# Attention and a squared-ReLU MLP on one core: two-unit cycles start two pairs earlier, and a batch's first product moves into the next batch's first two cycles

## Chip, core and metric

One core of one Trainium2 chip. The metric is the device time of one execution in microseconds, the median of several runs. The kernel before takes 417.85 us (417.56 to 418.05, four runs).

## The reference

```python
# q, k, v: 8 batches, 12 heads, 448 queries, 64 wide;  w_in: 768 x 2048;  w_out: 2048 x 768
scores = (1 / sqrt(64)) * q @ k.T
m = max(scores)                                   # by row
e = exp(scores - m)
attn = e / (sum(e) + exp(-m) + 1e-09)             # a "one" more in the denominator
x = (attn @ v)  as 3584 tokens x 768              # (batch, query) x (head, width)
out = relu(x @ w_in) ** 2 @ w_out
```

With exp(m) multiplied through, the denominator is the sum of exp(scores) plus one. The kernel computes it so, without the maximum.

## The kernel before, as far as the change touches it

A *unit* is a pair of heads with 448 queries (batch 0's are split into 192 and 256 queries). Per unit: eight score matmuls (in two halves, `c` = 0 and 1, two score tiles each), four exponentials on ScalarE, three adds on VectorE that shorten the row sums, values, row sums by TensorE, and a reciprocal made of two ScalarE instructions. The `..._psum` pools below hold TensorE's result tiles in PSUM, its result memory; a buffer can be written again once its reader is done. The *first product* (x @ w_in, 16 tiles of a batch's 448 tokens) and the *second product* (a *whole tile* is 128 tokens by 384 columns, 16 *pieces*) fill TensorE's time between them.

```python
s_psum = ctx.enter_context(tc.tile_pool(name="s_psum", bufs=2, ...))   # score tiles, 2 banks each
x_psum = ctx.enter_context(tc.tile_pool(name="x_psum", bufs=1, ...))
m_psum = ctx.enter_context(tc.tile_pool(name="m_psum", bufs=3, ...))
z_pool = ctx.enter_context(tc.tile_pool(name="z", bufs=2))             # reciprocals
...
def row_sums(us, sums):
    ...                                            # matmuls with ones into zp
    rcp = z_pool.tile([128, 512], FP32, name="rcp")
    nc.scalar.activation(out=rcp[:, 0:m], in_=zp[:, 0:m], func=AF.Ln, bias=one_b)
    nc.scalar.activation(out=rcp[:, 0:m], in_=rcp[:, 0:m], func=AF.Exp, scale=-1.0)
    return rcp
...
# one-unit cycles: batch 1, all six pairs (units 12 to 17)
for i in range(2 * NPAIR, 3 * NPAIR):
    ...                                            # scores, first product of batch 0, values, sums
    for step in range(3):
        add_chunks(u, et, es, half, step)          # VectorE's three adds
        drain(share[0] * (0.15, 0.1, 0.15)[step])  # some first product
    ...
# two-unit cycles: batches 2 to 7, three cycles each (pr = 0, 2, 4)
for c in range((NU - 3 * NPAIR) // 2):
    ...
    scores(ua, ea, 0)
    rows(11)                                       # 11 pieces of second product
    scores(ua, ea, 1)
    ...
    rows(11)
    scores(ub, eb, 0)
    ...
    rows(10)
    scores(ub, eb, 1)
    ...                                            # values and normalising of the cycle before
    if pr == 0:
        run(ins, len(ins))
        queue((b - 1) * S, S)                      # first product of the batch before
        if b > 2:
            run(outs)                              # one whole tile of second product
        ...
    n, early = ((3, 0 if b > 2 else 1), (7, 3), (6, 3))[pr // 2]
    run(ins, early)                                # tiles of first product
    for at in (i, i + 1):
        rcps[at] = row_sums([units[at]], (ess.pop(at)[0:1],))
    run(ins, n - early)
    if pr == NPAIR - 2:
        complete(b * S)                            # its second product may now start
```

## Time and profile before

| | before |
|---|---|
| median, us | 417.85 |
| span of the profiled execution, us | 415.9 |
| TensorE busy | 405.5 us (98%) |
| ScalarE busy | 238.4 us (57%) |
| start of batch 3, us | 116.53 |
| one batch in the steady part, us | 47.50 |
| from the last cycle's end (last values) to the end, us | 61.83 |

### The profile page before, as it was taken

What the parts mean: (1) busy time and instruction counts of PE and PEld (TensorE: products, weight loads), DVE (VectorE), ACT (ScalarE), POOL (GpSimd) and SP (SyncE); (2) the same over time, 40 slices, a digit from 0 to 9 for tenths busy, and PEclk for the clock granted to TensorE, in tenths of its full rate; (3) what the DMA queues carried; (4) which work ended last, traced back from release to release, by engine and by line L of the source; (5) the groups of instructions that cost most, each with busy time, mean ns of one, the idle gap of its engine ahead of it and who ended that gap; (6) DMA issues with size and microseconds to landing.
All of it is one profiled execution on the core that took longest, in us unless ns stands there. A gap on an engine that the chain in (4) does not pass through costs nothing.

```text
span 415.9 us, 10695 instructions
## 1 busy us (share of the span) xinstructions
PE 405.5 (98%) x4721; PEld 256.7 (62%) x4721; DVE 278.8 (67%) x535; ACT 238.4 (57%) x329; POOL 36.4 (9%) x58
## 2 busy tenths in 40 slices
PE   8889999899999999999999999999999999999997
PEld 3567666566566666665666666665666666555664
DVE  4769888768865868568766769658676669287000
ACT  4897998664675664673576564674666655100111
POOL 7523220020000200002000400001000000000000
PEclk9999999999999999999999999999999999999999
DMA  9999999889109790199509871198101101010222
GB/s 201 197 197 198 200 197 223 159 120 199 40 2 182 139 192 6 44 199 191 123 2 164 167 151 37 39 186 154 46 2 39 39 2 39 39 39 0 77 76 77
DMA packets 75823, 45.58 MB, mean 110 GB/s; under 512 B 42560, under 2 KB 72000, under 8 KB 75456
## 3 DMA queue, kind: packets, MB, share of 16 engines
q0 software_dynamic: 28848, 22.16, 35.0%
q1 hardware_dynamic: 46208, 22.05, 23.3%
q8 instruction: 37, 0.61, 0.6%
q10 hardware_dynamic: 720, 0.69, 0.6%
q14 instruction: 10, 0.08, 0.1%
HBM read 45.69 MB, written 17.93 MB: 153 GB/s over the span
## 4 chain that ended last, share of the span: by engine, by line
PE 86%; DMA 9%; ACT 2%; DVE 2%; issue 1%; POOL 0%; POOLq 0%
PE mp L284 23%; PE mp L330 17%; PE mp L286 11%; PE xp L284 8%; PE sp L199 6%; PE xp L330 6%; PE mp L234 5%; DMA kn<-in_k_dram 4%; PE xp L286 3%; DMA win<-in_moe_w_in_dram 3%; PE xp L234 3%; PE sp L187 2%; DMA vn<-in_v_dram 2%; PE mp L248 2%; ACT et L167 1%
## 5 line engine op out<-in xcount | busy, mean ns | idle before, releaser
L167 ACT ACTIVATE et<-sp 112x896 f16<-112x896 f32 (+2 forms) x192 | 165.8, 914 | 55.6 <-PE sp L199 40.1
L284 PEld LDWEIGHTS <-win 128*64 128x64 f16 x1536 | 85.3, 110 | 45.7 <-issue 2.8
L284 PE MATMUL mp<-xt,win 128*64 128x448 f16 (+2 forms) x1236 | 110.2, 324 | 1.5 <-DVE xt L263 0.8
L330 PE MATMUL mp<-wout,gs 64*128 64x384 f16 x864 | 102.3, 322 | 0.0
L330 PEld LDWEIGHTS <-gs 64*128 64x128 f16 x1152 | 56.1, 94 | 31.7
L301 DVE TENSOR_SCALAR rt<-mp 128x448 f16<-128x448 f32 (+2 forms) x99 | 61.6, 622 | 17.4 <-PE mp L284 13.3
L303 DVE TENSOR_TENSOR gs<-rt 128x448 f16<-128x448 f16 (+2 forms) x128 | 50.2, 392 | 4.4
L330 PE MATMUL xp<-wout,gs 64*128 64x384 f16 x288 | 52.6, 322 | 0.0
L251 ACT ACTIVATE rcp<-mp,one_b 128x448 f32<-128x448 f32 (+2 forms) x40 | 25.1, 629 | 40.1 <-PE mp L248 35.8
L212 DVE TENSOR_TENSOR es<-et 112x896 f16<-112x896 f16 x42 | 26.0, 620 | 17.7 <-ACT et L167 17.6
L339 ACT ACTIVATE ot<-mp 128x384 f32<-128x384 f32 (+1 forms) x29 | 14.1, 487 | 36.2 <-PE mp L286 27.6
L199 PE MATMUL sp<-qk 64*112 64x224 f16 x480 | 33.8, 260 | 0.0
L286 PEld LDWEIGHTS <-gs 128*128 128x128 f16 x256 | 24.4, 98 | 15.1 <-issue 0.4
L284 PE MATMUL xp<-xt,win 128*64 128x448 f16 x300 | 32.6, 352 | 0.0
L199 PEld LDWEIGHTS <-qk 64*112 64x112 f16 x480 | 26.3, 128 | 9.7 <-issue 5.4
L234 PEld LDWEIGHTS <-vn 112*64 112x64 f16 x432 | 22.1, 109 | 15.3 <-issue 5.2
L286 PE MATMUL mp<-wout,gs 128*128 128x384 f16 (+1 forms) x192 | 31.0, 322 | 0.0
L341 DVE SCALAR_TENSOR_TENSOR ot<-mp,ot 128x384 f32<-128x384 f32 x27 | 15.1, 558 | 21.7 <-PE sp L199 11.6
L252 ACT ACTIVATE rcp<-rcp 128x448 f32<-128x448 f32 (+2 forms) x48 | 27.7, 577 | 1.5
L214 DVE TENSOR_TENSOR es<-es,half 112x896 f16<-112x896 f16 x42 | 26.2, 625 | 1.4
L212 DVE TENSOR_TENSOR half<-et 112x896 f16<-112x896 f16 x42 | 25.9, 616 | 0.3 <-ACT et L167 0.3
L301 DVE TENSOR_SCALAR rt<-xp 128x448 f16<-128x448 f32 x29 | 18.0, 622 | 12.0 <-PE xp L286 8.3
(61 smaller groups left out, 313.9 us busy)
## 6 DMA issues: line engine op xcount, KB each, us to landing
vn<-in_v_dram POOLq DMA_DIRECT2D x7, 672.0 KB, 9.0
out_dram<-ot SPq DMA_DIRECT2D x9, 384.0 KB, 2.8
win<-in_moe_w_in_dram POOLq DMA_DIRECT2D x8, 384.0 KB, 13.9
wout<-in_moe_w_out_dram POOLq DMA_DIRECT2D x4, 768.0 KB, 12.8
stage_q<-in_q_dram POOLq DMA_DIRECT2D x4, 676.0 KB, 10.9
stage_k<-in_k_dram POOLq DMA_DIRECT2D x4, 676.0 KB, 13.3
out_dram<-ot SPq DMA_DIRECT2D x8, 288.0 KB, 3.2
out_dram<-ot SPq DMA_DIRECT2D x9, 192.0 KB, 2.7
```

What stands on the lines that cost most here:

```text
L167: nc.scalar.activation(out=out_, in_=in_, func=AF.Exp, scale=scale)
L199: nc.tensor.matmul(sp[:, odd, h * (S // 2):(h + 1) * (S // 2)], qk[r, which, kx:kx + 2 * P - 1:2], qk[r, 0, x:x + S // 2], start=True, sto ...
L212: nc.vector.tensor_add((es, half[:, 0:2 * S])[step], e[:, 2 * step], e[:, 2 * step + 1])
L214: nc.vector.tensor_add(es, es, half[:, 0:2 * S])
L234: nc.tensor.matmul(xp[64 * h:64 * h + 64, o:o + n], vns[b][:, 2 * pr + h, kk, :], of_head(chunk(et, u, kk // 2, kk), u, h), start=(kk == 0 ...
L251: nc.scalar.activation(out=rcp[:, 0:m], in_=zp[:, 0:m], func=AF.Ln, bias=one_b)
L252: nc.scalar.activation(out=rcp[:, 0:m], in_=rcp[:, 0:m], func=AF.Exp, scale=-1.0)
L284: nc.tensor.matmul(out_[x:x + 64], lhsT[:, x:x + 64], rhs, start=start, stop=stop)
L286: nc.tensor.matmul(out_, lhsT, rhs, start=start, stop=stop)
L301: nc.vector.tensor_scalar(out=rt[:, 0:m], in0=hp[:, 0:m], scalar1=0.0, scalar2=None, op0=ALU.max)
L303: nc.vector.tensor_mul(gs[:, f0:f0 + per, t0 % RING:t0 % RING + n], r, r)
L330: nc.tensor.matmul(o[:, 0:w], g[x:x + 64], wout[x:x + 64, fb, n0:n0 + w], start=(fb == 0), stop=(fb == NFFB - 1))
```

## The change

Its intent: the one-unit cycles are paced by ScalarE, and their only other work is what is left of batch 0's first product. The change shortens this stage from six units to four, and hands the last two pairs of batch 1 to the two-unit cycles, where second product fills TensorE. For there to be enough second product, a batch's first product has to be done a cycle earlier. So it all stands in the first two cycles of the next batch (8 and 8 tiles), the third has none, and the whole tile of second product goes there. VectorE's last two adds come a unit later, ahead of the sums that need them; values and sums stand before that unit's second scores and no longer behind them; and six of batch 0's 16 blocks are computed for all 448 tokens at once. The core of the diff:

```diff
-    for i in range(2 * NPAIR, 3 * NPAIR):
+    SINGLE = 2 * NPAIR + 4
+    ALONE = 10
+    def finish_sums(at):
+        for step in (1, 2):
+            add_chunks(units[at], ets[at], *ess[at], step)
+
+    for i in range(2 * NPAIR, SINGLE):
         ...
         scores(u, et, 0)
+        if not first:
+            finish_sums(i - 1)
         ...
-        drain(left() * 0.5 if first else share[0] * 0.45)
+        values(units[i - 1], ...); rcp = row_sums(...)
+        drain(left() if first else 450)
         scores(u, et, 1)
+        add_chunks(u, et, es, half, 0)
         if first:
+            normalise(done, xp, rcp)
+            queue(0, S, ALONE, NFFB)
+            queue(FIRST, S - FIRST, 0, ALONE)
+            drain(1850)
         else:
+            drain(600)
+            normalise(done, xp, rcp)
+            drain(1250)
 ... (cut: order of the loads; where the transposes stand)
-    for c in range((NU - 3 * NPAIR) // 2):
+    for c in range((NU - SINGLE) // 2):
         ...
         if pr == 0:
-            run(ins, len(ins))
             queue((b - 1) * S, S)
-            if b > 2:
-                run(outs)
-        n, early = ((3, 0 if b > 2 else 1), (7, 3), (6, 3))[pr // 2]
+        n, early = ((8, 3), (8, 3), (0, 0))[pr // 2] if c else (len(ins), 2)
         run(ins, early)
+        if c == 0:
+            normalise(units[i - 1:i], xp, rcps.pop(i - 1))
+            joined[0] = 0
+        elif pr == 4:
+            run(outs)
         for at in (i, i + 1):
             rcps[at] = row_sums([units[at]], (ess.pop(at)[0:1],))
         run(ins, n - early)
-        if pr == NPAIR - 2:
+        if c == 0 or pr == 2:
             complete(b * S)
```

More of the change, by code (lines that the diff above doesn't have):

```diff
@@ L374, with queue @@
     groups = [0]
-    def queue(t0, n):
+    def queue(t0, n, lo=0, hi=NFFB):
         per = max(1, 512 // n)
-        for f0 in range(0, NFFB, per):
+        for f0 in range(lo, hi, per):
             ns = per * DCH * n / 2.4
@@ L418 @@
     for pr in range(NPAIR):
-        transpose_at[NPAIR + 3 + pr] = (1, pr)
-    transpose_at[16], transpose_at[17] = (2, 0), (2, 1)
+        transpose_at[NPAIR + 3 + pr + pr // 3] = (1, pr)
+    SINGLE = 2 * NPAIR + 4
+    ALONE = 10
     def keep_warm(n):
@@ L463 @@
             normalise(two, xp, rcp)
-            queue(0, FIRST)
-            share[0] = left() / (NPAIR + 2)
+            queue(0, FIRST, 0, ALONE)
+            share[0] = left() / (NPAIR - 0.3)
         if i in transpose_at:
@@ L489 @@
         if i == NPAIR + 5:
+            for n0 in (0, HALF):
+                for j in range(2):
+                    load_wout(n0, j, 2)
             load_natural(2, 0, 3)
-            for j in range(2):
-                load_wout(0, j, 2)
-    for i in range(2 * NPAIR, 3 * NPAIR):
+    def finish_sums(at):
+        for step in (1, 2):
+            add_chunks(units[at], ets[at], *ess[at], step)
+    for i in range(2 * NPAIR, SINGLE):
         u, et, es, half = begin(i)
-        prev = units[i - 1]
         first = i == 2 * NPAIR
@@ L502 @@
         scores(u, et, 0)
+        if not first:
+            finish_sums(i - 1)
         if i in transpose_at:
             transposes(*transpose_at[i])
-        if i == 2 * NPAIR + 2:
-            load_natural(2, 3, 6)
-            for j in range(2):
-                load_wout(HALF, j, 2)
-            load_v(2, 0, 6)
-            stage(3)
-        drain(left() * 0.5 if first else share[0] * 0.45)
+        values(units[i - 1], ets.pop(i - 1), xp, units[i - 1][3] if first else 0)
+        done = units[i - 2:i] if first else units[i - 1:i]
+        rcp = row_sums(done, [ess.pop(units.index(d))[0:1] for d in done])
+        drain(left() if first else 450)
         scores(u, et, 1)
+        add_chunks(u, et, es, half, 0)
         if first:
-            done = units[i - 2:i]
-            values(prev, ets.pop(i - 1), xp, prev[3])
-            rcp = row_sums(done, (ess.pop(i - 2)[0:1], ess.pop(i - 1)[0:1]))
-        else:
-            done = [prev]
-            rcp = row_sums(done, (ess.pop(i - 1)[0:1],))
-            values(prev, ets.pop(i - 1), xp)
-        drain(share[0] * 0.15)
-        for step in range(3):
-            add_chunks(u, et, es, half, step)
-            drain(share[0] * (0.15, 0.1, 0.15)[step])
-        if i == 3 * NPAIR - 1 and ins and ins[0][0] < ins[0][1]:
-            run(ins)
-        normalise(done, xp, rcp)
-        if first:
-            queue(FIRST, S - FIRST)
-            share[0] = left() / (NPAIR + 1.5)
-    pending = [3 * NPAIR - 1]
-    joined[0] = 0
-    complete(S)
+            normalise(done, xp, rcp)
+            queue(0, S, ALONE, NFFB)
+            queue(FIRST, S - FIRST, 0, ALONE)
+            drain(1850)
+        else:
+            drain(600)
+            normalise(done, xp, rcp)
+            drain(1250)
+    if ins and ins[0][0] < ins[0][1]:
+        run(ins)
+    load_natural(2, 3, 6)
+    load_v(2, 0, NPAIR)
+    stage(3)
+    pending = [SINGLE - 1]
+    complete(128)
     def rows(n):
@@ L543, in rows @@
         mode[0] = COLS2
-    for c in range((NU - 3 * NPAIR) // 2):
-        i = 3 * NPAIR + 2 * c
+    for c in range((NU - SINGLE) // 2):
+        i = SINGLE + 2 * c
         b, pr = units[i][0:2]
-        new = []
-        for j in range(2):
-            new.append(begin(i + j))
-        (ua, ea, sa, ha), (ub, eb, sb, hb) = new
+        ua, ea, sa, ha = begin(i)
         scores(ua, ea, 0)
+        if c == 0:
+            finish_sums(i - 1)
         rows(11)
@@ L556 @@
         rows(11)
+        ub, eb, sb, hb = begin(i + 1)
         scores(ub, eb, 0)
@@ L563 @@
         mode[0] = COLS2
-        for at in pending:
-            if at not in rcps:
-                rcps[at] = row_sums([units[at]], (ess.pop(at)[0:1],))
-            xp = mp_tile()
-            values(units[at], ets.pop(at), xp)
-            normalise([units[at]], xp, rcps.pop(at))
+        if c == 0:
+            rcps[i - 1] = row_sums(units[i - 1:i], (ess.pop(i - 1)[0:1],))
+            xp = x_psum.tile([128, 512], FP32, name="xp")
+            values(units[i - 1], ets.pop(i - 1), xp)
+            transposes(2, 0)
+            transposes(2, 1)
+        else:
+            for at in pending:
+                xp = mp_tile()
+                values(units[at], ets.pop(at), xp)
+                normalise([units[at]], xp, rcps.pop(at))
         add_chunks(ub, eb, sb, hb, 1)
@@ L585 @@
                     stage(b + 2)
-        n, early = ((3, 0 if b > 2 else 1), (7, 3), (6, 3))[pr // 2]
+        n, early = ((8, 3), (8, 3), (0, 0))[pr // 2] if c else (len(ins), 2)
         run(ins, early)
+        if c == 0:
+            normalise(units[i - 1:i], xp, rcps.pop(i - 1))
+            joined[0] = 0
+        elif pr == 4:
+            run(outs)
         for at in (i, i + 1):
```

## The prediction

> **What bounds the kernel now.** I read first the page's table of engines, then the busy time by stretch with the cuts at the starts of the cycles, then TensorE's and ScalarE's timelines at two cycle borders, then the groups by shape.
>
> ```profile
> PE 405.5 (98%) x4721; PEld 256.7 (62%) x4721; DVE 278.8 (67%) x535; ACT 238.4 (57%) x329; POOL 36.4 (9%) x58
> ```
>
> TensorE is busy throughout, so a gain has to come out of its ten idle microseconds or out of matmuls that run slowly. The stretches say where these are (columns: span, then busy time of PE, PEld, DVE, ACT, POOL, clock, DMA share, GB/s).
>
> ```profile
> 45.13:65.40 20.27, 19.48 (x270) 13.09 (x271) 16.98 (x32) 18.93 (x26) 5.28 (x7) 1.00 1.34 199
> 67.35:83.11 15.76, 14.57 (x188) 9.51 (x186) 11.79 (x22) 10.69 (x15) 0.00 (x0) 1.00 0.87 177
> 83.11:100.83 17.72, 17.72 (x218) 11.41 (x216) 14.13 (x28) 9.58 (x13) 2.30 (x4) 1.00 1.00 175
> 100.83:116.53 15.70, 15.70 (x174) 9.32 (x172) 12.04 (x24) 9.58 (x13) 0.00 (x0) 1.00 0.15 43
> 116.53:131.45 14.92, 14.92 (x186) 9.60 (x184) 9.26 (x18) 9.96 (x14) 0.00 (x0) 1.00 0.45 73
> 131.45:148.31 16.86, 16.86 (x203) 10.68 (x201) 13.06 (x26) 9.59 (x13) 2.14 (x4) 1.00 0.97 178
> 148.31:164.03 15.72, 15.72 (x191) 9.97 (x189) 12.04 (x24) 9.58 (x13) 0.00 (x0) 1.00 0.35 83
> ```
>
> The first row is most of the one-unit cycles of batch 1 (a unit is a pair of heads, 448 queries): ACT is busy 18.93 of 20.27 us, so ScalarE is nearly the bound. The second is batch 2's first two-pair cycle, with 1.2 us of TensorE idle. From the third on TensorE never idles: the last three rows are one batch, 14.92 + 16.86 + 15.72 = 47.50 us, and every later batch repeats it. There any matmul, and any wait of a matmul, goes straight into the end. Now the border between two cycles, TensorE first, ScalarE second:
>
> ```profile
> 122.93 0.57 PE L199 MATMUL sp<-qk 64*112 64x224 f16 x8
> 123.43 1.70 PE L234 MATMUL mp<-et,vn 112*64 112x448 f16 x16
> 124.97 2.77 PE L284 MATMUL xp<-wout,gs 128*64 128x384 f16 x32
> 127.57 0.55 PE L248 MATMUL mp<-es,ones 112*64 112x448 f16 x4
> 127.95 1.30 PE L284 MATMUL mp<-xt,win 128*64 128x448 f16 x12
> 129.09 1.30 PE L284 MATMUL xp<-xt,win 128*64 128x448 f16 x12
> 130.22 1.30 PE L284 MATMUL mp<-xt,win 128*64 128x448 f16 x12
> 131.45 0.59 PE L199 MATMUL sp<-qk 64*112 64x224 f16 x8
> 133.67 0.55 PE L199 MATMUL sp<-qk 64*112 64x224 f16 x8
> ```
>
> ```profile
> 128.16 0.63 ACT L251 ACTIVATE rcp<-mp,one_b 128x448 f32<-128x448 f32 x1
> ...
> 129.95 0.58 ACT L252 ACTIVATE rcp<-rcp 128x448 f32<-128x448 f32 x1
> 131.90 1.72 ACT L167 ACTIVATE et<-sp 112x896 f16<-112x896 f32 x2 [1.36 <-PE sp L199]
> ```
>
> The row sums (L248) end at 127.95. ScalarE turns both into reciprocals, four instructions, until 129.95 + 0.58 = 130.53. Meanwhile TensorE does three tiles of the first product, 131.45 - 127.95 = 3.50 us, before the next scores. These tiles hide the reciprocals: the next exponentials find ScalarE idle for 1.36 us.
>
> **What the Trainium skill says.** "TensorE: Matmul & The Clock Gate", the table at its head, gives ScalarE a strict FIFO; so an exponential recorded after four reciprocals cannot overtake them. The trace agrees: ScalarE's starts above are in the program's order. The same page, "Back-to-back issue gap", puts a matmul at N/2.4 + 2.5 ns, 189 ns for 448 columns; here twelve 64-column halves (six products) take 129.09 - 127.95 = 1.14 us, 190 ns a product, so halves overlap and nothing is lost. "ScalarE: Activation LUTs", "What ACT_TABLE_LOAD costs", gives 186 + 0.833 N ns, 932 for N = 896; measured 914, and two in 1.72 us. "PSUM — Partial Sum Buffer", "Specifications", counts 8 banks: score tiles take 2 x 2, the value tile 1, the others 3, so a third score buffer has no room.
>
> **The change, part by part.** No arithmetic is added or removed: the built instruction orders differ only in place and shape. Four moves matter.
>
> (a) **Output work taken from the tail.** There are 19 two-pair cycles in place of 18 (32 pieces of second product each), and six extra whole tiles in place of five (16 pieces). So 32 + 16 = 48 pieces leave the tail, where 48 ran in 7.91 us: -7.8 us. They are done earlier, so this is no gain by itself; it must be set against what the earlier stages lengthen.
>
> (b) **Batch 0 and the four remaining one-unit cycles.** Batch 0's first half loses five first products of 192 columns in the cycles before (5 x 0.083 = 0.4 us); I take 0.3, so unit 12 starts at 36.9 and not 37.23. In unit 12 no product is left for the start, and the one-piece tiles need all of batch 0 normalised. Its exponentials run to 39.1, the reciprocals to 40.4, the VectorE multiply to 41.3; TensorE, done with the scores at 39.4, waits 1.9 us. Then 20 halves, and unit 13 starts at 43.3. Per unit afterwards: scores 2 x 0.5, transposes 0.42, values 0.75, sums 0.22, 28 to 30 halves about 2.8: 5.2 us, before 4.81. The late adds put two VectorE adds (2 x 0.63) in front of the sums, in line behind tile evictions of 1.0 us; I count waits of 0.7 and 0.8 us at the sums of units 13 and 14. Unit 14 starts at 48.5, unit 15 at 54.3. Unit 15 ends with 56 halves at 0.0545, 3.05 us. First two-pair cycle: 61.1.
>
> (c) **That cycle**: four score pitches with 32 pieces 6.9, sums and values 0.95, transposes 0.8, 48 halves 2.6, sums 0.4, and about 1.0 us waiting for a PSUM tile (the two-tile form uses three buffers there): it ends at 73.75. Then batch 2: its cycles have 8, 8 and 0 tiles of first product. A tile is 1.14 us. The first two are each the old row of 17.72 plus one tile, 18.86. The third is 14.92 less 3.50, about 11.45. With a border wait of 1.65 us (next paragraph) batch 3 begins at 73.75 + 1.65 + 18.86 + 18.86 + 11.45 = 124.6, before at 116.5: +8.1 us. So (a) to (c) sum to about +0.3: the work moved back in time is paid for fully.
>
> (d) **The border between a batch's third cycle and the next.** "First product in the first two cycles" takes away those three tiles. The order of the built program confirms it: second product (32 halves), sums, then scores at once; and on ScalarE four reciprocals, then six exponentials. Shift the quoted trace by 3.50 us: scores at 127.95, their exponentials wanted at 128.40, ScalarE free at 130.43. The first exponential ends at 131.35, the second at 132.2. The second pair of score tiles, due at 127.95 + 2.22 = 130.17, needs these buffers; its last four matmuls start at about 132.2, not 130.37. So TensorE stands still about 2.0 us, and later intervals of 2.17 us against 1.72 give nothing back. This comes at five borders (batches 2|3 to 6|7): +10.0 us. A batch is 18.0 + 18.0 + 11.45 + 2.0 = 49.5 in place of 47.5.
>
> Sum: +0.3 + 10.0 = 10.3, 428 us. As (b) and (c) were walked with every wait against the kernel, I take one off: **427 us**.
>
> **The rivals.** *The intended one: the stage bound by ScalarE shrinks from six units to four and TensorE fills.* For it: ScalarE's 18.93 of 20.27. If (b) and (c) had no wait at all, unit 12 to batch 3 would take 3.7 + 5.2 + 5.2 + 6.2 + 12 + 49.2 = 81.5 us, batch 3 would begin at 118.4 and, less 7.8 us, the time would be 6 us better: 412 without the border waits, 422 with them. Against it: TensorE already did 19.48 of 20.27 there. *The border wait is smaller.* If sums of the first unit come early or an eviction moves, 1 us each gives 422. *Transfers.* The second product's weights now go ahead of batch 2's queries; before, they were needed at 67.8 and now at 61.5. Four loads of 768 KB at 199 GB/s take 3.9 us each, an estimate; behind batch 1's values, which landed at about 42, they end near 58. It fits, with 3 us to spare; if it doesn't, 430.
>
> **Range and chances.** The low end, 421, is nearly all of the intended gain with most of the border waits; the high end, 431, is my walk with further waits in (b). Two per cent above is 426.2, just below my figure: slower 0.57, within 2% 0.40, faster 0.03, which would need the border waits not to exist.
>
> **What would show it.** In the new profile: each first cycle of batches 3 to 7 has idle TensorE time of about 2 us before its second scores, released by ScalarE's exponential; a batch takes 49.5 us; the tail loses 7.8 us; TensorE's idle or stretched time sits in units 12 to 15 too, and the first two-pair cycle starts near 61. The prediction is wrong if batches still take 47.5 us, if the two-pair cycles begin by 58, or if the first output rows wait for a load.

## The result, and the profile after

427.06 us (427.02 to 427.19, four runs) against 417.85: the ratio is 1.0222, 95% interval 1.0204 to 1.0239, slower. (A ratio is taken from the runs of the same rounds, so it is not quite the ratio of the medians.) The page's table of engines:

```profile
PE 406.7 (96%) x4697; PEld 264.9 (62%) x4697; DVE 280.7 (66%) x538; ACT 236.4 (56%) x328; POOL 36.2 (9%) x58
```

TensorE does the same work in a span of 425.3 us and idles eight microseconds longer. The stretches, cut at the starts of the stages, with the columns of the prediction's view:

```profile
42.11:60.41 18.30, 17.07 (x228) 10.19 (x226) 15.39 (x30) 13.56 (x18) 3.47 (x5) 1.00 1.35 202
60.41:73.45 13.04, 12.23 (x176) 8.65 (x174) 9.94 (x19) 8.40 (x12) 0.00 (x0) 1.00 1.24 217
73.45:94.34 20.89, 19.61 (x230) 13.48 (x228) 15.50 (x30) 11.70 (x17) 0.00 (x0) 1.00 0.59 115
94.34:113.20 18.86, 18.86 (x230) 12.28 (x229) 15.15 (x30) 9.59 (x13) 2.13 (x4) 1.00 0.77 148
113.20:124.69 11.49, 11.49 (x135) 7.05 (x133) 7.25 (x14) 7.54 (x10) 0.00 (x0) 1.00 0.14 36
124.69:144.53 19.84, 18.48 (x216) 13.53 (x214) 13.04 (x25) 11.78 (x18) 0.37 (x1) 1.00 0.66 125
```

They are: one-unit cycles (units 13 to 15); the first two-unit cycle; batch 2's three cycles; batch 3's first. The fourth row is a cycle with eight tiles and no wait, 18.86 us; the third is the same work with 20.89, and the last has 1.36 us of idle TensorE. This is what stands at that border, TensorE first and then ScalarE:

```profile
121.61 2.77 PE L284 MATMUL mp<-wout,gs 128*64 128x384 f16 x32
124.21 0.55 PE L248 MATMUL mp<-es,ones 112*64 112x448 f16 x4
124.69 0.59 PE L199 MATMUL sp<-qk 64*112 64x224 f16 x8
128.03 0.40 PE L199 MATMUL sp<-qk 64*112 64x224 f16 x4 [0.96 <-ACT et L167]
128.84 0.40 PE L199 MATMUL sp<-qk 64*112 64x224 f16 x4 [0.41 <-ACT et L167]
130.81 0.60 PE L199 MATMUL sp<-qk 64*112 64x224 f16 x8
```

```profile
124.42 0.49 ACT L339 ACTIVATE ot<-mp 128x384 f32<-128x384 f32 x1 [2.54 <-PE mp L284]
124.81 0.63 ACT L251 ACTIVATE rcp<-mp,one_b 128x448 f32<-128x448 f32 x1
...
126.60 0.58 ACT L252 ACTIVATE rcp<-rcp 128x448 f32<-128x448 f32 x1
127.08 3.32 ACT L167 ACTIVATE et<-sp 112x896 f16<-112x896 f32 x4
```

The scores follow the sums at once. ScalarE evicts the whole tile, makes two reciprocals, and begins the exponentials at 127.08, 2.39 us after the scores began. The second scores need the first ones' two buffers and get them one by one, at 128.03 and 128.84. From the first scores to the third it takes 130.81 - 124.69 = 6.12 us. In the kernel before, the scores at this border were

```profile
116.53 0.59 PE L199 MATMUL sp<-qk 64*112 64x224 f16 x8
118.75 0.55 PE L199 MATMUL sp<-qk 64*112 64x224 f16 x8
120.92 0.55 PE L199 MATMUL sp<-qk 64*112 64x224 f16 x8
```

or 120.92 - 116.53 = 4.39. The border costs 1.73 us; of this, 0.96 + 0.41 us show as idle time of TensorE. Over the whole span, TensorE's waits for an exponential in these batches (columns: total us, times, longest us) are

```profile
PE sp L199 <- ACT et L167: 6.8, 10, 1.0
```

two at each of five borders; the kernel before has no wait of TensorE between 116 and 354 us.

Where the difference of the spans, 425.3 - 415.9 = 9.4 us, comes from:

| stage | before, us | after, us | difference | predicted |
|---|---|---|---|---|
| start to batch 3 | 116.53 | 124.69 | +8.16 | +8.1 |
| batches 3 to 7 | 237.54 (47.5 each) | 246.46 (49.3 each) | +8.92 | +10.0 |
| last values to the end | 61.83 | 54.15 | -7.68 | -7.8 |

The first and last rows belong together: 48 pieces of second product left the tail and are done before batch 3.

### The profile page after: what moved, and what is told of

The parts are those of the page before. It is cut to its first block, busy times and chain, and to the rows that moved or that the text cites. A ratio compares the mean times of both kernels' runs of the same rounds, so it can differ in the third digit from the quotient of the medians. Undisturbed runs are those within 1.5% of the kernel's fastest.

```text
span 425.3 us, 10659 instructions
## 1 busy us (share of the span) xinstructions
PE 406.7 (96%) x4697; PEld 264.9 (62%) x4697; DVE 280.7 (66%) x538; ACT 236.4 (56%) x328; POOL 36.2 (9%) x58
## 4 chain that ended last, share of the span: by engine, by line
PE 84%; ACT 9%; DVE 4%; issue 1%; DMA 1%; ACTq 0%
PE mp L284 25%; PE mp L330 16%; PE mp L286 9%; PE xp L284 7%; PE sp L199 5%; ACT et L167 5%; PE mp L234 5%; PE xp L330 5%; PE xp L234 3%; PE xp L286 3%; PE sp L187 3%; ACT rcp L251 2%; PE mp L248 2%; ACT rcp L252 1%; PE mp L156 1%
## 5 line engine op out<-in xcount | busy, mean ns | idle before, releaser
L330 PE MATMUL mp<-wout,gs 64*128 64x384 f16 x928 | 109.0, 322 | 0.5 <-DVE ot L337 0.5
L330 PEld LDWEIGHTS <-gs 64*128 64x128 f16 x1216 | 65.7, 94 | 29.8 <-issue 1.8
L199 PE MATMUL sp<-qk 64*112 64x224 f16 x480 | 35.6, 260 | 6.8 <-ACT et L167 6.8
L339 ACT ACTIVATE ot<-mp 128x384 f32<-128x384 f32 (+2 forms) x28 | 13.4, 480 | 50.3 <-PE mp L286 36.6
L199 PEld LDWEIGHTS <-qk 64*112 64x112 f16 x480 | 27.6, 128 | 17.4 <-issue 14.1
L341 DVE SCALAR_TENSOR_TENSOR ot<-mp,ot 128x384 f32<-128x384 f32 x29 | 16.2, 558 | 24.3 <-PE sp L199 11.6
L284 PE MATMUL xp<-xt,win 128*64 128x448 f16 x288 | 31.5, 353 | 0.0
L286 PEld LDWEIGHTS <-gs 128*128 128x128 f16 x208 | 19.7, 98 | 12.0 <-issue 0.4
L187 PE MATMUL sp<-qk 64*112 64x448 f16 (+2 forms) x192 | 23.5, 319 | 1.4 <-ACT et L167 0.9
L286 PE MATMUL mp<-wout,gs 128*128 128x384 f16 (+2 forms) x160 | 24.3, 310 | 0.0
```

The costliest lines, as they stand in the source:

```text
L187: nc.tensor.matmul(sp[:, h, o:o + n], qk[r, 1, x + P * kk:x + P * kk + P], qk[r, 0, x + q0:x + q0 + n], start=True, stop=True)
L199: nc.tensor.matmul(sp[:, odd, h * (S // 2):(h + 1) * (S // 2)], qk[r, which, kx:kx + 2 * P - 1:2], qk[r, 0, x:x + S // 2], start=True, sto ...
L284: nc.tensor.matmul(out_[x:x + 64], lhsT[:, x:x + 64], rhs, start=start, stop=stop)
L286: nc.tensor.matmul(out_, lhsT, rhs, start=start, stop=stop)
L330: nc.tensor.matmul(o[:, 0:w], g[x:x + 64], wout[x:x + 64, fb, n0:n0 + w], start=(fb == 0), stop=(fb == NFFB - 1))
```

## The experiments

They go after three questions: is it the border, and through ScalarE's reciprocals; what is the front (all before batch 3) worth alone; and which of the front's waits cost anything. Each run's ratio is to the kernel before in the same rounds.

### Undo the cost: reciprocals on VectorE

```diff
+        if on_vector:
+            nc.vector.tensor_scalar(out=rcp[:, 0:m], in0=zp[:, 0:m], scalar1=1.0 / GS, scalar2=None, op0=ALU.add)
+            nc.vector.reciprocal(out=rcp[:, 0:m], in_=rcp[:, 0:m])
+            return rcp
...
-            rcps[at] = row_sums([units[at]], (ess.pop(at)[0:1],))
+            rcps[at] = row_sums([units[at]], (ess.pop(at)[0:1],), on_vector=pr == 4)
```

> The changed kernel, with the reciprocals of each third cycle of batches 2 to 7 computed by VectorE (one add, one reciprocal, VectorE stands idle there) in place of four ScalarE instructions. Theory (the reciprocals stand in ScalarE's FIFO ahead of the next exponentials, and TensorE waits 1.73 us at each of five borders): the wait vanishes, 5 x 1.73 = 8.7 us less, about 418.4 us. Rival (TensorE waits at the border for another reason, say the sums, the switch of array halves or the score buffers as such): no change, 427.

Measured: 433.61 us, ratio 1.0385, so neither theory's number. (The edit also met the first two-unit cycle, seven cycles in all.) The group of the new instruction says why:

```profile
L253 DVE RECIPROCAL rcp<-rcp 128x448 f32<-128x448 f32 x14 | 41.3, 2953 | 0.5
```

One VectorE reciprocal takes 2.95 us, five times an add, and 41.3 us in all. VectorE then came late with its evictions and multiplies: behind batch 3's first scores its two reciprocals ran until 133.9, and over the run TensorE waited longest in the first product for VectorE's multiplies (4.4 us) and in the rows for these reciprocals' adds, which free a PSUM tile (2.2 us). But at this border the second scores started 129.13 - 126.91 = 2.22 us after the first, the undisturbed interval. At this border the wait went, and larger ones came elsewhere. The run's time therefore says nothing of what the border costs; a fix with cheaper means was needed.

### Halve the cost: one pair of reciprocals beside the tile

```diff
-        elif pr == 4:
-            run(outs)
         for at in (i, i + 1):
+            if at == i + 1 and c and pr == 4:
+                run(outs)
             rcps[at] = row_sums([units[at]], (ess.pop(at)[0:1],))
```

> The changed kernel, with the first unit's sums put ahead of the whole output tile in the third cycle and the second unit's left behind it, so that one pair of reciprocals (1.2 us) runs beside the tile. Theory: each border wait falls from 1.73 to about 0.55 us, 5 x 1.17 = 5.9 us less, about 421.2 us. Rival (the wait does not come from the length of the reciprocals): 427, or more if the early sums wait for VectorE's adds.

Measured: 422.44 us, ratio 1.0118: 4.6 us less than the changed kernel, predicted 5.9. The scores of the same border:

```profile
124.83 0.59 PE L199 MATMUL sp<-qk 64*112 64x224 f16 x8
127.23 0.40 PE L199 MATMUL sp<-qk 64*112 64x224 f16 x4
128.04 0.40 PE L199 MATMUL sp<-qk 64*112 64x224 f16 x4 [0.41 <-ACT et L167]
...
130.02 0.60 PE L199 MATMUL sp<-qk 64*112 64x224 f16 x8
```

130.02 - 124.83 = 5.19, a delay of 0.80 in place of 1.73; 5 x 0.93 = 4.65 us. The wait follows what ScalarE has still to do after the sums.

### The split alone, in the kernel before

```diff
-            if b > 2:
-                run(outs)
...
-        n, early = ((3, 0 if b > 2 else 1), (7, 3), (6, 3))[pr // 2]
+        n, early = ((8, 3), (8, 3), (0, 0))[pr // 2]
         run(ins, early)
+        if pr == 4:
+            run(outs)
...
-        if pr == NPAIR - 2:
+        if pr == 2:
             complete(b * S)
```

> The kernel before, with only the new split of the first product over a batch's cycles (8, 8, 0 tiles, the whole output tile in the third cycle). Its front is the old one. Theory (the loss is the border's): 417.85 + 5 x 1.73 = 426.5 us. Rival (the loss is the new front's, batch 0's and 1's cycles): 418 us.

Measured: 426.32 us, ratio 1.0211 (1.0195 to 1.0226), 8.6 us above the kernel before. The view's line for the scores' waits is the changed kernel's, word for word: 6.8 us in total, ten times, the longest 1.0 us. This one part of the change brings nearly all of its loss, without a line of the new front, for which 9.2 - 8.6 = 0.6 us is left.

### The front alone, with the old split

```diff
+        if b == 2 and pr == 4:
+            run(ins, 1)
         rows(10)
+        if b == 2 and pr == 4:
+            run(ins, 1)
...
+            if b > 2:
+                run(outs)
...
-        n, early = ((8, 3), (8, 3), (0, 0))[pr // 2] if c else (len(ins), 2)
+        n, early = ((3, 0 if b > 2 else 1), (7, 3), (4, 1) if b == 2 else (6, 3))[pr // 2] if c else (len(ins), 2)
...
-        elif pr == 4:
-            run(outs)
...
-        if c == 0 or pr == 2:
+        if c == 0 or pr == 4:
             complete(b * S)
```

> The changed kernel's front (two-pair cycles from batch 1's last two pairs, late sums, batch 0 partly in one piece), with the old split of the first product (3, 7, 6 tiles); as batch 1's output is then not ready in batch 2's third cycle, two of that cycle's tiles stand where the missing output rows stood. Theory (the front alone is worth about +0.3 us: 8.1 us later at batch 3 less 7.8 us of tail): 417.5 to 419 us. Rival 1 (the front is what costs): 425 or more. Rival 2 (the front alone gives the intended gain): 412 to 415.

Measured: 424.11 us, ratio 1.0153, which fits none of the three. I had miscounted: of batch 0's 448 tokens only three whole groups of 128 are complete, 96 pieces, and the three cycles before had used them all. Batch 2's third cycle had not 16 pieces but none, and its four scores stood side by side:

```profile
107.18 0.58 PE L187 MATMUL sp<-qk 64*112 64x448 f16 x4
108.58 0.40 PE L187 MATMUL sp<-qk 64*112 64x448 f16 x2 [0.82 <-ACT et L167]
```

That cycle took 16.0 us (107.18 to 123.21) and did no second product; batch 3 began 123.21 - 116.53 = 6.7 us later than before with as many pieces done, about the 6.4 us by which the run is longer. The run is inconclusive for the front. It does show that this front needs the new split: with the old one there was no second product for the extra cycle.

### The border covered

```diff
-        if rows and n0 == 0:
+        if (rows and n0 == 0) or vector_evicts[0]:
             nc.vector.tensor_scalar(...)
         else:
             nc.scalar.activation(...)
...
-        elif pr == 4:
-            run(outs)
         for at in (i, i + 1):
+            if at == i + 1 and c and pr == 4:
+                for _ in range(12):
+                    one(outs)
             rcps[at] = row_sums([units[at]], (ess.pop(at)[0:1],))
+        if c and pr == 4:
+            vector_evicts[0] = True
+            run(outs)
+            vector_evicts[0] = False
```

Each `one(outs)` issues one of the tile's 16 pieces; with `vector_evicts` VectorE, not ScalarE, copies the tile out.

> The changed kernel, with the third cycle's border covered: first unit's sums ahead of the whole output tile, second unit's after 12 of its 16 pieces, the tile's eviction on VectorE. ScalarE then has its last pair of reciprocals done about 0.3 us after the next exponentials could start. Theory (the five border waits are the loss of the steady part): they fall from 1.73 to about 0.15 us each, 7.9 us less, 419.2 us, and batches take 47.5 to 47.7 us. What stays above the kernel before, about 1.3 us, is then the front. Rival (the run with the first unit's sums moved gained for another reason, such as one switch of array halves less): about 422, as there.

Measured: 418.83 us, ratio 1.0027 (1.0018 to 1.0037). The scores at the border of batches 2 and 3:

```profile
125.03 0.59 PE L199 MATMUL sp<-qk 64*112 64x224 f16 x8
127.24 0.55 PE L199 MATMUL sp<-qk 64*112 64x224 f16 x8
129.41 0.55 PE L199 MATMUL sp<-qk 64*112 64x224 f16 x8
```

129.41 - 125.03 = 4.38: the border wait is gone, and no wait of these scores for an exponential is left in the profile. 8.2 of the 9.2 us are settled by this. Of the 1.0 us that remains, about half is still in batches 3 to 7: in the profile they run from 125.03 to 363.05, 47.6 us each against 47.5 before. The other half, by subtraction, is the front with its own border before batch 2, against the predicted 0.3.

### Three attempts in the front

The first undoes the late adds alone, in the changed kernel:

```diff
-        if not first:
+        if i == 2 * NPAIR + 1:
             finish_sums(i - 1)
...
             normalise(done, xp, rcp)
+            finish_sums(i)
             drain(1250)
...
-        if c == 0:
-            finish_sums(i - 1)
```

> The changed kernel with one part of it undone: VectorE's two last adds of units 13 to 15 stand in their own unit again, ahead of its last tile evictions. In the changed kernel TensorE waits 0.64 us at the sums of unit 13 and 0.59 at those of unit 14 for these adds, and ScalarE 0.7 us each. Theory (both stand on the path of that stage): these waits go and about 1.2 us with them, 425.9 us. Rival (evictions are now late instead, or ScalarE's exponentials take up the time): 427 us.

Measured: 427.19 us, ratio 1.0222: nothing. The waits for the adds were real,

```profile
PE mp L248 <- DVE es L214: 1.2, 2, 0.6
```

in the changed kernel, but with the adds ahead it is the evictions of first-product tiles that come late. TensorE waited in the next matmuls, 0.50 us where it had waited 0.64:

```profile
49.36 0.35 PE L248 MATMUL mp<-es,ones 112*64 112x448 f16 x2
50.21 0.76 PE L284 MATMUL mp<-xt,win 128*64 128x448 f16 x6 [0.50 <-DVE rt L301]
```

and the second of the waits became 0.16, with 0.28 more at the first rows; ScalarE, which had gained time at the sums, gave it back at the next scores. Counted from unit 12's first scores (36.98 here, 36.68 in the changed kernel, though up to there the programs are the same), the first two-unit cycle began 0.57 us earlier, but its second scores came 2.66 us after its first and not 2.21, and batch 2's second scores came only 0.13 us earlier.

The second moved the first unit's sums of the first two-unit cycle ahead of that cycle's tiles:

> The border covered, and in the very first two-pair cycle the first unit's sums ahead of that cycle's two tiles of first product, so that its reciprocals run beside them. There the second scores of the next cycle came about 1.4 us late. Theory: 1.2 us less than with the border alone, about 418.0 us. Rival (that cycle's wait has other owners, such as the PSUM tile that waits for a VectorE multiply, 0.67 us): 419.2.

Measured: 419.10 us, ratio 1.0029, the same as with the border alone. The second unit's reciprocal started 1.6 us after its sums were done, when ScalarE had been idle for 3.13 us:

```profile
75.09 0.63 ACT L251 ACTIVATE rcp<-mp,one_b 128x448 f32<-128x448 f32 x1 [3.13 <-DVE xt L260]
```

It writes a reciprocal buffer, there are two, and this one was free only when VectorE had multiplied unit 15's values, recorded behind the evictions of both tiles. The two attempts together, on top of the covered border, gave the same:

> All three together: border covered, sums of the first two-pair cycle's first unit ahead of its tiles, adds in their own unit. Theory: 419.2 - 1.2 - 1.2 = 416.8 us, under the kernel before. Rival (the front's waits replace each other): 418 to 419.

Measured: 418.81 us, ratio 1.0029.

The third takes that knowledge: on top of the covered border, the multiply goes ahead of the tiles, and one of unit 15's tiles of first product goes behind this cycle's sums.

```diff
-            drain(1250)
+            drain(1250 if i < SINGLE - 1 else 0)
...
+        if c == 0:
+            normalise(units[i - 1:i], xp, rcps.pop(i - 1))
         run(ins, early)
         if c == 0:
-            normalise(units[i - 1:i], xp, rcps.pop(i - 1))
             joined[0] = 0
```

> The border covered as before, and the same done for the first two-pair cycle in another way: one 256-column tile of first product less at the end of unit 15, where ScalarE stood idle 1.71 us, and one more behind that cycle's sums, with the multiply that frees the reciprocals' buffer ahead of the tiles. In the changed kernel the second scores of the next cycle came 2.0 us late there (6.39 us where undisturbed cycles have 4.39). Theory: the wait falls to about 0.3 us, 1.7 us less than with the border alone, 417.1 us, just under the kernel before. Rival (the tile moved out of unit 15 uncovers a wait there, as with the other two attempts in the front): 418.8.

Measured: 417.54 us (21 runs), before 417.80, ratio 0.9996 (0.9990 to 1.0003). Batch 2's first scores stand at the undisturbed interval again:

```profile
74.81 0.58 PE L187 MATMUL sp<-qk 64*112 64x448 f16 x4
77.02 0.54 PE L187 MATMUL sp<-qk 64*112 64x448 f16 x4
```

The edit was worth 1.3 us, predicted 1.7, by the medians 418.83 and 417.54.

A last one kept ten products of batch 0 for unit 12, by a share of `left() / (NPAIR + 1.0)` in place of `left() / (NPAIR - 0.3)`:

> As the run with the first cycle covered, and ten products of batch 0's first half kept for unit 12, which has none in the changed kernel; TensorE waits there 0.40 us for an add and 0.69 us for the normalising multiply, and some more inside its scores. Theory: the ten products (0.8 us, taken from the cycles before) run in these waits, 0.5 to 0.8 us less, 416.4 us. Rival (the cycles before are paced by VectorE and don't get shorter, or the late tile's eviction delays the multiply): no change.

Measured: 417.45 us (14 runs, one of them 420.19 at a clock of 0.992), ratio 1.0001 (0.9989 to 1.0012): no change that these runs can tell. In the profile the products do run in unit 12 and its wait for the adds is gone, but the wait for the multiply is still 0.78 us, and earlier cycles show a new 1.11 us wait of scores for an exponential. So the best that the change came to here is the kernel before's time, with nothing gained.

## Why the prediction was right

**The border, step (d), is shown.** The scores come at once after the sums, ScalarE's reciprocals stand ahead of the exponentials, and the second scores wait for the buffers. The split alone in the old kernel gave 426.32 us; halving the reciprocals behind the sums halved the delay, from 1.73 to 0.80 us; covering them removed it and 8.2 us. The size was put a little high: 2.0 us a border where 1.73 was measured between the scores, and 49.5 us a batch where 49.3 was measured. The term mis-sized is when ScalarE gets free: 2.39 us after the scores, predicted 2.48; and the last step was rounded up, from 132.2 - 130.37 to 2.0. In the table above the five batches came out 1.1 us below the prediction, which is about the difference between the sum of 10.3 and the measured 9.2. The one microsecond taken off for caution was meant for (b) and (c), which needed none, and happened to match the excess in (d). That 427.0 met 427.06 to a tenth is therefore luck in part.

**The front, steps (b) and (c), was right in sum: batch 3 at 124.69, predicted 124.6.** The terms were less exact, in both directions. Unit 12 waited 0.69 us for the multiply, not 1.9, because eight of its halves work on pairs that had been normalised before and ran first, and the multiply was done at 40.80, not 41.3; unit 13 began at 42.11, not 43.3. Units 14 and 15 then took 6.04 and 6.99 us from scores to scores, predicted 5.8 and 6.8, and the border before batch 2 cost 2.0 us, not 1.65. (The prediction takes the 1.65 from its paragraph (d), which has 2.0 and never derives it.) ScalarE waited there 0.35 us for a reciprocal buffer that I had not counted. The first two-unit cycle began at 60.41, predicted 61.1, and took 13.04 us, predicted 12.65. That such terms added up to the right tenth is luck too. The waits at the sums of units 13 and 14, 0.64 and 0.59 us against 0.7 and 0.8, were there, but the run without them shows that they were not worth their length, though the walk had assumed so.

**The tail, step (a):** -7.68 us, predicted -7.8.

**The rivals.** The intended gain exists only on paper: with both borders covered the kernel equals the one before. TensorE's 19.48 of 20.27 us in the old one-unit cycles was the sign, for the view shows only 0.8 us of idle time in that stretch. In the new units 13 to 15 TensorE is busy 17.07 of 18.30, no better. The weights' loads were in time: they landed between 19 and 25 us after issue at 26.7 to 33.1, the last at 57.6 at the latest by adding these, and the first rows at 60.84 waited for none.

**What the Trainium skill said** held in the new trace: ScalarE's order, named in "TensorE: Matmul & The Clock Gate", table at its head, is one half of the mechanism, and the two score buffers are the other; the exponentials start at 127.08 although their scores were done about two microseconds before. Of the other statements that the prediction draws on, that page gives N/2.4 + 2.5 ns as the gap of an isolated matmul, which the prediction leaves out, so it is the trace's 190 ns a product that carries the argument; and no run here tests the count of eight PSUM banks.

## What to carry to other kernels

Work that looks like filler between two steps of a pipeline may hide a third engine's latency; before it is moved, ask which waits it covers, and leave that engine's queue of in-order work clear at that place. Where a filler must go, a remedy is to move the in-order work ahead of what is left: sums in two parts, each with something behind it, together with the tile's copy on another engine, gave back 8.2 us here. A wait seen in a profile is worth its length only if nothing stands ready to take its place; in the front, removing the waits for the adds moved nothing, and only covering the border before batch 2 moved the end.

## What the Trainium skill lacked or had wrong

- "VectorE: DVE Perf Modes", "First, the fixed hardware budget", says that a reciprocal repeats its divide steps eight times, and I found no duration for it there or on the other VectorE pages. Measured: 2.95 us for 128 x 448 in fp32, 2953 / 448 = 6.6 ns a column, against 0.60 us for an add and 0.62 for a multiply of the same shape. A line with that number would have spared a run.
- "ScalarE: Activation LUTs", "What ACT_TABLE_LOAD costs": 186 + 0.833 N gives 932 ns for N = 896; measured 914. With a pointer operand, 280 + 0.833 N gives 653 for N = 448; the logarithm with its bias took 628. Both are 2 to 4% high for these shapes.
- "TensorE: Matmul & The Clock Gate", Part 3, tells how row and column tiles run beside each other; I found no figure there, nor on the page about array packing, for a change from one to the other in a stream. Here the next matmul starts 0.39 us after the scores begin when it too is split by rows (118.75 to 119.14), and 0.50 us when it is split by columns (122.93 to 123.43), so about 0.1 us for this change, an estimate from these two places, which no run isolates.
